# Splitting the first token-pair loads of a recurrence-and-mixer kernel between two issuing engines

## The chip, the core and the metric

The kernel runs on one core of a Trainium2 chip. The metric is the device time of one execution in microseconds (us). Beside plain runs there is one profiled execution, whose trace names every instruction, its engine and what it waited for.

## What is computed

The program is a gated linear recurrence followed by a token mixer and a channel MLP. Cut to what matters:

```python
# q, k, v, alpha: batch 4, heads 8, tokens 768, head size 48
for t in range(S):
    state = alpha[:, :, t, :, None] * state + einsum('bhd,bhe->bhde', k[:, :, t], v[:, :, t])
    y[:, :, t] = einsum('bhd,bhde->bhe', q[:, :, t], state)
x  = y with heads side by side            # (4, 768, 384)
u  = x + (x^T @ U @ V)^T                   # U: 768 x 32, V: 32 x 768
out = u + relu(u @ w_ch1) @ w_ch2          # 384 -> 1536 -> 384
```

## The kernel before

The 768 tokens of each batch are cut into six chunks of 128 tokens, written here as batch.chunk (q 1.1 is the q tensor of batch 1, chunk 1). A chunk needs four inputs: `alpha`, `k`, `q` and `v`, each 192 KB of float32 in one tile of a pool of 40 tiles named `io`. The 24 weight pieces (12 of `moe_w_ch1`, 12 of `moe_w_ch2`, also 192 KB each) and the results use the same pool.

Two forms of chunk exist. In batch 0 (all six chunks) and batch 1 (the first four) chunks are *paired*: a partition holds two neighbouring tokens of four heads, and the load reads runs of two tokens (line 322, "pload"). These are the token-pair loads, 40 in all; two of the first 36 are issued by ScalarE, the rest by SyncE. The other chunks are loaded a token to a partition (line 329).

For a paired chunk (`stage_pair`): ScalarE takes the logarithm of alpha (line 352); TensorE sums it over the tokens (lines 361 to 368); ScalarE takes exponentials (lines 375 to 377); VectorE or GpSimd multiply q and k by them (line 383, tile `rkq`); TensorE transposes both (line 400) and ScalarE or VectorE copy the result to `kqt`; TensorE forms the scores (line 424), VectorE masks them (line 435, tile `pm`), TensorE forms the state's increment (line 458), and the outputs (lines 497 and 507), which go to `xb` by way of `copy` (lines 263 to 267). `stage_mix` then builds u (lines 674 to 689) and its transpose `uT` (line 708), and `mlp1` and `mlp2` are the two large products (lines 737 and 763). Weight pieces are loaded at line 295 and cast to bf16 by `copy`.

The order of everything is written out by hand: `TABLE` is a string of three characters for each operation. The first two give the operation's number in base 64, the third the engine that runs it (P TensorE, A ScalarE, D VectorE, G GpSimd, S SyncE). `Plan.run` walks through it and emits the operations in that order; `SLOTS` gives the pool slot that each buffer takes when it is first used:

```python
op = self.ops[CODE.index(table[n]) * len(CODE) + CODE.index(table[n + 1])]
...
op.fn({"P": "PE", "A": "ACT", "D": "DVE", "G": "POOL", "S": "SP"}[table[n + 2]])
```

A load takes its issuing engine from that third letter:

```python
lambda e: (nc.scalar if e == "ACT" else nc.sync).dma_start(
    t().rearrange("p (h j) d -> p h (j d)", j=2), src[b, hs, sl, :].rearrange("h (p j) d -> p h (j d)", j=2)
),
```

Each engine works through its own list in that order. Waits between engines, and between a load and an earlier one that used the same semaphore, are put in when the program is built; loads and stores use eight semaphores (named DMAHW0 to DMAHW7 in the built program).

Of the kernel before, what the change touches and what calls it, by code (L numbers as in the profile page):

```python
# [13 lines left out]

CODE = "ABCDEFGHIJKLMNOPQRSTUVWXYZabcdefghijklmnopqrstuvwxyz0123456789+-"
TABLE = """
BISA8ABASA-AQgAA9SDjAA+SDlPBQSCcACePBKSCzABCSBBSC1PCdACfAABSChACgADnABDSCjDC4AC3ABJSCiDETABES++EClPDqGCkPBMSCnDEVPBRSC6G
CmDDsPBLSEYAC2ACrPDuABSSC5GCoPCsDDmABOSC8PEWACpDAFGC7PC0ABHSCtPCvPCqDC+ADCPDpGDKAC9DBFSCuDEXAC-PDDDBYSCwPEZGDADDEPDrPBUS
DMPDBDDtADkGDGPBGSDNACxDEaGDHPDFDDPADOADvPCyDBTSD8AEbPDIDDyPDJDDLGEcPDoADwDDZPD+PEeAEdDAGPEAABNSDzPDxDAHAEfPBPSD0DDQGEhD
BWSEDGGTABVSDaPAJPGqADbDAASDSPDRGD1PD-AGVPDUDEBAAKADcPD2DGsPGXADdDEUGDTPEgDGWABXSD3PECGEiPD4PEFPGuADVDEjPGtAD5PEHDD9GGvA  # L20
DWPGYABZSD7AGaGD6AEEPEkDElPBgSDYDELPEmPEGADePEMPBaSDXDGZGDfPEIPBcSENDDgPEJDADGEnPBbSDhAEPPGcPEpAEKDGbPDiAAQSEOPGUAEQPEoD
AMSGdAGeDGiPGwGERDEqPAOSESAGjDGfPHaAErPGkDGmPGyPGgDEsAGxGAUSHcPGhDASSE1PE7PHfAG0AE5PAWSE2DGnPHBAEzPE6DBdSGrGGpAGzPGoAEvP
E8DAeSG1AEtPHDPE0DAaSARAANGE9PEuDHGABeSE3PAPGE+AEwDG5PBkSG2PE4DHFAAVGAiSG6DExPHeAFXPHEAATGEyDFZPAXGG7DG9PFYDAgSFBPGlGG4D
FfPAfGFCAE-PHHDFgAAYSFJPG3DHdABiSFAAFdPBoSFaAFFPHIGFeDFKAAcSFhPFGAFHPHzABhSFDPFiAAhGBmSAjAH1PAZGFEDFbPBfSG8GH3AHJPH4AHKP
HhGFcAHLDFrPBlSFIAHMDFTPFsDFVPFUAAdGBjSHVPAbAHNPFWDHgGG+PHPDAmSFtPG-AH2AHODHjPH7GHAAFnPBqSIJAHlDFlPH5AAqSHCGFuDILPHiPFmD
AkSFRPINAH6GFoDHkAFjPFSAAoSHQPFkAHmPBpSHRDIMAH9PHoDH8PAwSHSGH-AFNPHbGHnDAySH+AHWPFpPFOAHTDIPGBnSHXPIAPAsSHYDHpPHZAICDFLP
# [802 lines left out]
```

## Time and profile before

| | |
|---|---|
| Runs | 159.76 us median of 3 (158.51 to 160.31) |
| Profiled execution | 158.96 us, of which the span of the trace is 157.2 us |
| Busy in the span | TensorE 147.3, VectorE 107.0, ScalarE 87.2, GpSimd 64.6 us |
| Moved | 31.64 MB, of which 28.62 MB on SyncE's queue (q1) and 2.75 MB on ScalarE's (q10) |
| Granted TensorE clock | full speed in every slice |

In the rows of the profile PE is TensorE, PEld its weight loads, DVE VectorE, ACT ScalarE, POOL GpSimd and SP SyncE. A name with a q (SPq, ACTq) is that engine's own list of instructions, on which loads are issued; the duration of such a row is the time of issuing, with any wait for a semaphore, and not that of the transfer. "To landing" is the time from the start of issuing until the data are there. Busy time of TensorE counts matmuls that overlap in its pipeline, so a row's mean is longer than the step from one matmul to the next.

### The profile page before, as it was taken

How to read it: one execution, taken by the hardware profiler on the slowest of the kernel's cores; microseconds unless marked ns; L12 is line 12 of the kernel's file. 1: busy time of each engine (PE TensorE's matmuls, PEld its weight loads, DVE VectorE, ACT ScalarE, POOL GpSimd, SP SyncE). 2: the span in 40 equal slices, each digit the busy share in tenths (PEclk: the TensorE clock that was granted, in tenths of full speed). 3: DMA queues.
4: the chain of work that ended last, by engine and by line, in shares of the span. 5: the costliest groups of instructions: out<-in, count | busy, mean ns of one | idle time of the engine just before them, and what ended most of it. 6: DMA issues, size and time to landing. Idle time of an engine off the chain costs nothing.

```text
span 157.2 us, 4460 instructions
## 1 busy us (share of the span) xinstructions
PE 147.3 (94%) x1708; PEld 97.5 (62%) x1708; DVE 107.0 (68%) x235; ACT 87.2 (55%) x226; POOL 64.6 (41%) x103
## 2 busy tenths in 40 slices
PE   0898998899999999999999999999999999999991
PEld 0567785566666656667667766666667565566561
DVE  6159998883878658986985948775798463435152
ACT  3858877869797636659788473358713102460000
POOL 8069865656868050275289246155412000000000
PEclk9999999999999999999999999999999999999999
DMA  5999889999999999899999899599780056875234
GB/s 124 323 327 320 230 198 253 277 311 278 251 264 293 246 266 219 151 200 238 206 238 169 139 231 135 116 209 217 145 198 23 0 104 160 263 222 135 74 126 174
DMA packets 99364, 31.64 MB, mean 201 GB/s; under 512 B 93040, under 2 KB 99312, under 8 KB 99344
## 3 DMA queue, kind: packets, MB, share of 16 engines
q1 hardware_dynamic: 85808, 28.62, 77.9%
q10 hardware_dynamic: 13536, 2.75, 9.1%
q8 instruction: 13, 0.21, 0.6%
q14 instruction: 7, 0.06, 0.1%
HBM read 23.89 MB, written 4.72 MB: 182 GB/s over the span
## 4 chain that ended last, share of the span: by engine, by line
PE 77%; SPq 14%; DMA 3%; ACT 1%; issue 1%; POOL 1%; DVE 1%; ACTq 0%
PE ps L763 30%; PE ps L737 29%; SPq L322 12%; DMA io<-in_alpha_dram 3%; PE ps L592 2%; PE ps L564 2%; PE ps L688 2%; PE ps L659 2%; PE ps L530 1%; PE ps L654 1%; PE ps L615 1%; PE ps L708 1%; SPq L270 1%; PE ps L674 1%; PE ps L400 1%
## 5 line engine op out<-in xcount | busy, mean ns | idle before, releaser
L763 PE MATMUL ps<-w_sb,h1t 128*128 128x384 bf16 (+2 forms) x300 | 53.2, 320 | 0.0
L737 PE MATMUL ps<-uT,w_sb 128*128 128x384 bf16 x288 | 51.2, 326 | 0.0
L747 ACT ACTIVATE h1t<-ps 128x384 bf16<-128x384 f32 x57 | 25.9, 501 | 20.9 <-PE ps L737 20.9
L763 PEld LDWEIGHTS <-h1t 128*128 128x128 bf16 x300 | 27.2, 97 | 16.1 <-issue 1.0
L737 PEld LDWEIGHTS <-w_sb 128*128 128x128 bf16 x288 | 27.0, 98 | 16.0
L749 DVE TENSOR_SCALAR h1t<-ps 128x384 bf16<-128x384 f32 x39 | 20.8, 554 | 12.5 <-PE ps L737 12.2
L769 DVE TENSOR_TENSOR io<-ub,ps 128x384 f32<-128x384 bf16 (+2 forms) x25 | 13.2, 536 | 11.3 <-PE ps L763 10.6
L602 DVE TENSOR_TENSOR pm<-ps,maskc 128x512 bf16<-128x512 f32 x28 | 17.7, 683 | 1.0 <-PE ps L592 0.8
L551 POOL TENSOR_TENSOR rkq<-io,ai 128x384 bf16<-128x384 f32 x11 | 10.2, 935 | 14.2 <-DMA io<-in_k_dram 6.6
L689 DVE TENSOR_TENSOR ub<-xb,ps 128x384 bf16<-128x384 bf16 x24 | 12.1, 551 | 2.8 <-PE ps L688 2.7
L551 POOL TENSOR_TENSOR rkq<-io,aa 128x384 bf16<-128x384 f32 x12 | 10.9, 912 | 7.1 <-PE ps L763 3.5
L435 DVE TENSOR_TENSOR pm<-ps,maskp 128x512 bf16<-128x512 f32 x20 | 13.1, 684 | 0.3
L263 ACT CAST xb<-ps 128x192 bf16<-128x192 f32 (+1 forms) x24 | 9.1, 402 | 5.9 <-DVE io L769 2.5
L383 POOL TENSOR_TENSOR rkq<-io,aa 128x384 bf16<-128x384 f32 x9 | 8.2, 918 | 9.2 <-ACT aa L376 4.1
L263 ACT COPY kqt<-ps 128x512 bf16<-128x512 bf16 x18 | 10.5, 595 | 1.5 <-PE ps L400 0.7
L626 POOL TENSOR_TENSOR st<-sm,tot 128x384 bf16<-128x384 f32 x6 | 5.0, 828 | 12.7 <-DVE sm L642 10.7
L267 POOL CAST w_sb<-io 128x384 bf16<-128x384 f32 x16 | 8.1, 514 | 4.6 <-DMA io<-in_moe_w_ch_dram 4.4
L541 ACT ACTIVATE aa<-ps 128x384 bf16<-128x384 f32 x14 | 6.9, 504 | 5.1 <-PE ps L532 4.4
L543 ACT ACTIVATE tot<-ps,off 128x4 f32<-128x4 f32 x22 | 5.9, 278 | 6.4 <-PE ps L532 6.4
L267 POOL CAST rv<-io 128x384 bf16<-128x384 f32 x17 | 8.8, 526 | 1.2 <-DMA io<-in_v_dram 1.1
L265 DVE COPY kqt<-ps 128x512 bf16<-128x512 bf16 x18 | 7.4, 418 | 2.9 <-PE ps L564 1.3
L400 PE MATMUL ps<-ident,rkq 128*128 128x128 bf16 x80 | 8.0, 232 | 1.3 <-ACT lt L352 0.6
(109 smaller groups left out, 214.8 us busy)
## 6 DMA issues: line engine op xcount, KB each, us to landing
io<-in_k_dram SPq DMA_DIRECT2D x24, 192.0 KB, 4.1
io<-in_q_dram SPq DMA_DIRECT2D x24, 192.0 KB, 4.4
io<-in_moe_w_ch_dram SPq DMA_DIRECT2D x24, 192.0 KB, 3.9
io<-in_alpha_dram SPq DMA_DIRECT2D x23, 192.0 KB, 4.2
io<-in_v_dram ACTq DMA_DIRECT2D x13, 192.0 KB, 4.2
out_dram<-io SPq DMA_DIRECT2D x13, 192.0 KB, 2.0
io<-in_v_dram SPq DMA_DIRECT2D x11, 192.0 KB, 3.8
out_dram<-io SPq DMA_DIRECT2D x20, 96.0 KB, 2.2
```

Of the source, the lines that this page charges most:

```text
L263: nc.scalar.copy(dst, src)
L267: nc.gpsimd.tensor_copy(dst, src)
L322: lambda e: (nc.scalar if e == "ACT" else nc.sync).dma_start(t().rearrange("p (h j) d -> p h (j d)", j=2), src[b, hs, sl, :].rearrange("h ...
L435: nc.vector.tensor_tensor(dst, s2, maskp.to_broadcast([C, 2, 2, C]), op=ALU.mult)
L551: eng.tensor_tensor(dst()[:, :, 0:D], a(), x(), op=ALU.mult)
L602: nc.vector.tensor_tensor(pm()[:, :, par, :], s2, maskc.to_broadcast([C, HP, C]), op=ALU.mult)
L689: P.add(f"u {b}.{c}", lambda e, c=c, hb=hb: nc.vector.tensor_tensor(ub()[:, c, :], xb()[:, c, :], hb()[:, 0:DM], op=ALU.add), r=[hb] + xk( ...
L737: nc.tensor.matmul(hb()[:, 0:TW], lhsT=w1_sb[:, ct, jt * 128 : (jt + 1) * 128], rhs=u_half(uT, ct, tt, b in QUEUE_U), start=(ct == 0), sto ...
L747: nc.scalar.activation(dst, hb()[:, 0:TW], AF.Relu)
L749: nc.vector.tensor_scalar_max(dst, hb()[:, 0:TW], 0.0)
L763: nc.tensor.matmul(hb()[:, 0 : hi - lo], lhsT=h1()[:, jt, c * C : (c + 1) * C], rhs=w2_sb[:, jt, lo:hi], start=(jt == 0), stop=(jt == NJ - 1),
L769: P.add(f"out_{hi - lo} {b}.{c}", lambda e, hb=hb, lo=lo, hi=hi: nc.vector.tensor_tensor(flat(ou)[:, lo:hi], ub()[:, c, lo:hi], hb()[:, 0 ...
```

## The change

Every second of the first 36 token-pair loads has the letter A in the place of S. Sixteen letters change; the two loads that were ScalarE's already keep theirs, so that 18 of the 36 are ScalarE's. The places in the table, the slots and all other operations stay. The moved loads, in the table's order, are q 0.0, q 0.3, k 0.1, k 0.3, alpha 0.4, v 0.3, q 0.4, k 0.2, alpha 1.0, v 0.5, v 0.4, k 1.0, k 1.1, q 1.1, v 1.1 and q 1.2. In the table:

```diff
-BISA8ABASA-AQgAA9SDjAA+SDlPBQSCcACePBKSCzABCSBBSC1PCdACfAABSChACgADnABDSCjDC4AC3ABJSCiDETABES++EClPDqGCkPBMSCnDEVPBRSC6G
-CmDDsPBLSEYAC2ACrPDuABSSC5GCoPCsDDmABOSC8PEWACpDAFGC7PC0ABHSCtPCvPCqDC+ADCPDpGDKAC9DBFSCuDEXAC-PDDDBYSCwPEZGDADDEPDrPBUS
+BISA8ABASA-AQgAA9SDjAA+ADlPBQSCcACePBKACzABCSBBAC1PCdACfAABSChACgADnABDSCjDC4AC3ABJACiDETABES++EClPDqGCkPBMACnDEVPBRSC6G
+CmDDsPBLAEYAC2ACrPDuABSSC5GCoPCsDDmABOAC8PEWACpDAFGC7PC0ABHSCtPCvPCqDC+ADCPDpGDKAC9DBFACuDEXAC-PDDDBYSCwPEZGDADDEPDrPBUA
...
```

The next rows of the table change alike: `BTS` (v 0.5), `BPS` (v 0.4), `BVS` (k 1.0), `BZS` (k 1.1), `BaS` (q 1.1), `BbS` (v 1.1) and `BeS` (q 1.2) end in A. The lists of TensorE, VectorE and GpSimd stay as they are; ScalarE's has 16 loads more and SyncE's 16 fewer.

More of the change, by code (lines that the diff above doesn't have):

```diff
@@ L16 @@
 TABLE = """
-BISA8ABASA-AQgAA9SDjAA+SDlPBQSCcACePBKSCzABCSBBSC1PCdACfAABSChACgADnABDSCjDC4AC3ABJSCiDETABES++EClPDqGCkPBMSCnDEVPBRSC6G
-CmDDsPBLSEYAC2ACrPDuABSSC5GCoPCsDDmABOSC8PEWACpDAFGC7PC0ABHSCtPCvPCqDC+ADCPDpGDKAC9DBFSCuDEXAC-PDDDBYSCwPEZGDADDEPDrPBUS
-DMPDBDDtADkGDGPBGSDNACxDEaGDHPDFDDPADOADvPCyDBTSD8AEbPDIDDyPDJDDLGEcPDoADwDDZPD+PEeAEdDAGPEAABNSDzPDxDAHAEfPBPSD0DDQGEhD
-BWSEDGGTABVSDaPAJPGqADbDAASDSPDRGD1PD-AGVPDUDEBAAKADcPD2DGsPGXADdDEUGDTPEgDGWABXSD3PECGEiPD4PEFPGuADVDEjPGtAD5PEHDD9GGvA
-DWPGYABZSD7AGaGD6AEEPEkDElPBgSDYDELPEmPEGADePEMPBaSDXDGZGDfPEIPBcSENDDgPEJDADGEnPBbSDhAEPPGcPEpAEKDGbPDiAAQSEOPGUAEQPEoD
+BISA8ABASA-AQgAA9SDjAA+ADlPBQSCcACePBKACzABCSBBAC1PCdACfAABSChACgADnABDSCjDC4AC3ABJACiDETABES++EClPDqGCkPBMACnDEVPBRSC6G
+CmDDsPBLAEYAC2ACrPDuABSSC5GCoPCsDDmABOAC8PEWACpDAFGC7PC0ABHSCtPCvPCqDC+ADCPDpGDKAC9DBFACuDEXAC-PDDDBYSCwPEZGDADDEPDrPBUA
+DMPDBDDtADkGDGPBGSDNACxDEaGDHPDFDDPADOADvPCyDBTAD8AEbPDIDDyPDJDDLGEcPDoADwDDZPD+PEeAEdDAGPEAABNSDzPDxDAHAEfPBPAD0DDQGEhD
+BWSEDGGTABVADaPAJPGqADbDAASDSPDRGD1PD-AGVPDUDEBAAKADcPD2DGsPGXADdDEUGDTPEgDGWABXSD3PECGEiPD4PEFPGuADVDEjPGtAD5PEHDD9GGvA
+DWPGYABZAD7AGaGD6AEEPEkDElPBgSDYDELPEmPEGADePEMPBaADXDGZGDfPEIPBcSENDDgPEJDADGEnPBbADhAEPPGcPEpAEKDGbPDiAAQSEOPGUAEQPEoD
 AMSGdAGeDGiPGwGERDEqPAOSESAGjDGfPHaAErPGkDGmPGyPGgDEsAGxGAUSHcPGhDASSE1PE7PHfAG0AE5PAWSE2DGnPHBAEzPE6DBdSGrGGpAGzPGoAEvP
-E8DAeSG1AEtPHDPE0DAaSARAANGE9PEuDHGABeSE3PAPGE+AEwDG5PBkSG2PE4DHFAAVGAiSG6DExPHeAFXPHEAATGEyDFZPAXGG7DG9PFYDAgSFBPGlGG4D
+E8DAeSG1AEtPHDPE0DAaSARAANGE9PEuDHGABeAE3PAPGE+AEwDG5PBkSG2PE4DHFAAVGAiSG6DExPHeAFXPHEAATGEyDFZPAXGG7DG9PFYDAgSFBPGlGG4D
 FfPAfGFCAE-PHHDFgAAYSFJPG3DHdABiSFAAFdPBoSFaAFFPHIGFeDFKAAcSFhPFGAFHPHzABhSFDPFiAAhGBmSAjAH1PAZGFEDFbPBfSG8GH3AHJPH4AHKP
```

## The prediction

> **What bounds the kernel now.** I read the chain that ended last first, then the chain in order of time, then the busy time by stretch, then the engines' own rows around 28 us. The page's chain:
>
> ```profile
> PE 77%; SPq 14%; DMA 3%; ACT 1%; issue 1%; POOL 1%; DVE 1%; ACTq 0%
> PE ps L763 30%; PE ps L737 29%; SPq L322 12%; DMA io<-in_alpha_dram 3%; PE ps L592 2%; PE ps L564 2%; PE ps L688 2%; PE ps L659 2%; PE ps L530 1%; PE ps L654 1%; PE ps L615 1%; PE ps L708 1%; SPq L270 1%; PE ps L674 1%; PE ps L400 1%
> ```
>
> Two stages show here: a long one that TensorE sets, and an opening whose chain is SyncE issuing the token-pair loads (line 322). In order of time the opening ends so (start us, us, what):
>
> ```profile
> 23.42 5.30 DMA io<-in_alpha_dram
> ```
>
> and at the same moment GpSimd waits for the q load that was issued just before (start, duration, engine, line, what; in brackets the idle time and what ended it):
>
> ```profile
> 28.37 0.91 POOL L383 TENSOR_TENSOR rkq<-io,aa 128x384 bf16<-128x384 f32 x1 [2.60 <-DMA io<-in_q_dram]
> ```
>
> The busy time by stretch (stretch: length, PE, PEld, DVE, ACT, POOL busy, granted clock, DMA share, GB/s):
>
> ```profile
> 7.90:15.70 7.80, 7.20 (x145) 5.50 (x144) 5.78 (x15) 5.40 (x16) 6.53 (x8) 1.00 1.17 323
> 15.70:23.60 7.90, 7.90 (x190) 6.17 (x188) 7.66 (x20) 6.42 (x21) 5.98 (x10) 1.00 0.86 214
> 23.60:31.40 7.80, 6.51 (x136) 4.50 (x129) 6.82 (x16) 6.00 (x17) 4.49 (x7) 1.00 0.97 265
> 31.40:120.00 88.60, 88.38 (x989) 58.03 (x986) 67.08 (x132) 57.85 (x150) 44.23 (x65) 1.00 1.02 210
> 120.00:157.20 37.20, 33.99 (x244) 21.01 (x240) 16.45 (x33) 6.76 (x16) 0.13 (x1) 1.00 0.47 133
> ```
>
> The reader is to see three things. After 31.4 us TensorE is busy 88.38 of 88.60 us and its order is fixed, so a microsecond lost before 31.4 is hardly ever given back, and one gained there is kept. In the opening no engine has much room: VectorE 7.66 of 7.90, ScalarE 6.42 of 7.90. And 323 GB/s over 7.8 us looks like the ceiling of the transfers: a load of 192 KB (196.6 thousand bytes) takes 0.61 us of it.
>
> **What the change does to the order.** Of the 36 loads two were ScalarE's already; sixteen more go there. The change keeps each load's place in the program, but an engine works through its own list. SyncE loses sixteen items and runs ahead, into the weight loads; a load on ScalarE goes out only when ScalarE has come to it. Beyond that, the compiled program gives the loads eight semaphores in turn and lets each load wait until the one eight places ahead has landed, over both queues. The places are those of the build's merged order, and that order has changed (places from 0, read from the two compiled programs; chunks are written batch.chunk):
>
> ```
> load     place before -> after   after: waits for place
> v 0.5        24 -> 33             25 (second half of U)
> v 0.4        26 -> 39             31 (first weight)
> k 1.0        28 -> 42             34 (weight)
> k 1.1        32 -> 48             40 (weight)
> q 1.1        34 -> 51             43 (alpha of a single chunk)
> v 1.1        36 -> 53             45 (weight)
> alpha 1.2    35 -> 30             22 (q 0.4)
> 1st weight   37 -> 31             23
> ```
>
> So the last pair loads that the opening needs stand 13 to 17 places later, behind weights that nobody needs yet, and the waiting instruction is on ScalarE: every activation and copy behind it waits too.
>
> **The terms.** What SyncE did, and what a landing takes:
>
> ```profile
> 2.33 0.51 SPq L322 DMA_DIRECT2D io<-in_q_dram  x1
> ...
> 14.28 1.15 SPq L322 DMA_DIRECT2D io<-in_v_dram  x1
> ...
> 21.77 0.51 SPq L322 DMA_DIRECT2D io<-in_k_dram  x1
> ...
> 22.87 0.51 SPq L322 DMA_DIRECT2D io<-in_q_dram  x1
> ```
>
> ```profile
> DMA to landing us min/median/max: 2.9/4.2/5.3
> ```
>
> An issue without a wait takes 0.51 us; the one of 1.15 holds a wait for a semaphore.
>
> *Issuing on ScalarE.* Sixteen times 0.51 is 8.2 us of ScalarE's sequencer. ScalarE has issued loads before:
>
> ```profile
> 52.41 0.52 ACT L263 CAST w_sb<-io 128x384 bf16<-128x384 f32 x1
> 52.55 0.40 ACTq L329 DMA_DIRECT2D io<-in_v_dram  x1
> 52.82 0.52 ACT L263 CAST rv<-io 128x384 bf16<-128x384 f32 x1
> ```
>
> The two casts start 0.41 us apart with an issue of 0.40 us between: it ran under the first cast. The bounds are 0 and 8.2 us; I take 0 by this row, since nearly every moved issue follows an activation of about 0.5 us that covers it. Without that cover (ScalarE waiting, queue empty) each costs its 0.51. SyncE's saved 8.2 us are worth nothing by themselves while the transfers are at their ceiling.
>
> *The start.* q 0.0 went out at 2.33; now it follows the first Ln on ScalarE.
>
> ```profile
> 3.98 0.94 ACT L352 ACTIVATE lt<-io 128x384 bf16<-128x384 f32 x2 [0.82 <-DMA io<-in_alpha_dram]
> 7.25 0.56 DVE L383 TENSOR_TENSOR rkq<-io,aa 128x384 bf16<-128x384 f32 x1 [3.05 <-ACT aa L376]
> ```
>
> 4.0 + 4.2 = 8.2 against VectorE's start at 7.25: the first product is 0.95 us late. It is no term of its own: the later hold is longer, and takes its place.
>
> *The hold on ScalarE.* I carry every load through the rule "issued when its engine is there and the load eight places ahead has landed", with 4.2 us to land and 0.55 us between SyncE's issues. The rows of ScalarE that tell when it would be there:
>
> ```profile
> 11.29 0.90 ACT L375 ACTIVATE ai<-ps 128x384 bf16<-128x384 f32 x2
> ...
> 15.27 0.51 ACT L376 ACTIVATE aa<-ps 128x384 bf16<-128x384 f32 x1
> 15.64 0.54 ACT L352 ACTIVATE lt<-io 128x384 bf16<-128x384 f32 x1
> ...
> 18.21 0.94 ACT L352 ACTIVATE lt<-io 128x384 bf16<-128x384 f32 x2 [0.40 <-DMA io<-in_alpha_dram]
> ...
> 23.51 0.78 ACT L263 CAST xb<-ps 128x192 bf16<-128x192 f32 x3 [0.95 <-PE ps L507]
> ...
> 26.47 0.52 ACT L352 ACTIVATE lt<-io 128x384 bf16<-128x384 f32 x1 [0.71 <-DMA io<-in_alpha_dram]
> ...
> 28.80 0.52 ACT L352 ACTIVATE lt<-io 128x384 bf16<-128x384 f32 x1 [0.47 <-DMA io<-in_alpha_dram]
> ```
>
> q 0.0 goes out at 4.0 and lands at 8.2; q 0.5 on SyncE waits for it and lands at 12.4; q 0.4 on ScalarE waits for that one, where ScalarE would have been after the first Exp of 11.29, at 11.7: about +1.0 with the issue. v 0.5 waits for the second U load, issued 13.5, landed 17.7, where ScalarE stands at 16.6 with that delay (15.27, 0.4 and 1.0): the Ln of 15.64 starts at 17.75 (+2.1). v 0.4 waits for the first weight, issued 17.15, landed 21.35: the Ln of 18.21 at 21.4 (+3.2). k 1.0 waits for a weight issued 18.3: 22.5 (+3.9). k 1.1: 26.1 for 21.77. q 1.1: 27.25 for 22.87. v 1.1: 28.35; the casts of 23.51 begin at 28.4 (**+4.9**). q 1.1 then lands at 31.45, where GpSimd began with it at 28.37 (+3.1). Behind the last cast stand the mixer's first product, the chain to `uT` and the first MLP matmul:
>
> ```profile
> 32.42 1.14 PE L737 MATMUL ps<-uT,w_sb 128*128 128x384 bf16 x6
> ```
>
> Of the two alpha waits above (0.71 and 0.47) those loads, now early, give back about 0.7. With 4.2 us a landing the opening ends **4.2 us** late.
>
> *Is 4.2 right?* In that order eight loads are nearly always under way: 8 x 196.6 / 4.2 gives 374 GB/s, more than the 323 that the rows reach. At 323 GB/s place 43, for which q 1.1 waits, lands no sooner than 3.9 + 43 x 0.61 - 1.1 (three loads are short) = 29.0, q 1.1 itself at 33.2: 4.8 late. And in the middle of the opening a landing took longer:
>
> ```profile
> io<-in_alpha_dram SPq DMA_DIRECT2D x4, 192.0 KB, 5.1
> ```
>
> (alpha loads issued from 12 to 24 us: their number, size, median us to landing). v 1.1 stands behind six landings in a row on its semaphore, so 0.1 us more on each is 0.6 us at the end. With 4.4 the end is 1.2 later than with 4.2: 5.4; 4.8 by the ceiling; I take **+5.5** for the opening with the queue at its ceiling, and nothing back later, since TensorE is busy 88.38 of 88.60 us. Bounds: 3.7 us a landing gives 4.2 - 3.0 = +1.2; 4.9 gives 4.2 + 4.2 = +8.4.
>
> *Sum.* The profiled execution took 158.96 us: 158.96 + 5.5 = 164.5 us. The median of the runs shown is 159.76, 0.8 above it; I leave the sum where it is. One per cent, about what a measurement of this kernel tells from no change, is 1.6 us.
>
> **Rivals.**
>
> *SyncE freed: faster.* The chain of the opening is SyncE's issues; with half of them gone alpha 1.2 goes out near 16.6 and not at 23.42, the weights come early, and TensorE's gaps before 31.4 close. They are 0.60 + 0 + 1.29 us in the three stretches after 7.9: 158.96 - 1.9 = 157.1. It decides if ScalarE is never held for over about 1 us, the slack of 0.95 it has at 23.51. For it: the alpha row of 5.30 us. Against it: the q that comes at the same moment is ScalarE's now, and the transfers are at 323 GB/s. [...] Chance 0.04.
>
> *ScalarE's loads land sooner.* A second queue with one or two loads in it might be served ahead of its share, so that landings fall to 3.6 us: 4.9 - 6 x 0.6 = +1.3 on ScalarE, 160.3. The rows so far speak against it:
>
> ```profile
> io<-in_v_dram ACTq DMA_DIRECT2D x13, 192.0 KB, 4.2
> ...
> io<-in_v_dram SPq DMA_DIRECT2D x11, 192.0 KB, 3.8
> ```
>
> [...] Chance 0.10.
>
> *The hold feeds itself.* ScalarE late makes its loads late, SyncE's loads wait for those, and landings stay near the 5.1 of the middle, at 5.0: 4.2 + 6 x 0.8 = +9, 168.0, more if the second batch's loads follow. For it: 214 GB/s between 15.7 and 23.6, with waits for semaphores on SyncE. Against it: once ScalarE is held, fewer loads are under way. Chance 0.10.
>
> **How the numbers follow.** The forecast has the remaining 0.76, with its own range 161.0 to 167.5. The range for 8 in 10 is 160.8 to 168.8: it holds the forecast and most of the self-feeding hold, and leaves out the faster rival and the quick landings (0.14) and the far end. Faster by over 1%: 0.03, all from the first rival. Within 1%: 0.09, 0.01 from the first and 0.08 from the second. Slower: 0.88.
>
> **What would show it.** Right: ScalarE issues on its queue of well over 1 us between 15 and 30 us, k 1.1, q 1.1 and v 1.1 issued after 25 us, the alpha load of 1.2 and the first weights issued before 19 us, GpSimd waiting for k and q of 1.1, the first MLP matmul near 38 and not 32.4, and nearly the same time from there to the end. Wrong: ScalarE's issues all near 0.5 us, or VectorE and TensorE no later at 30 us than before; or landings well under 4 us; or a late opening that is made up before 120 us.

## The result, and the profile after

The changed kernel takes 167.84 us (median of 4 runs, 166.57 to 168.13); the kernel before took 160.03 beside it (158.51 to 160.63). The ratio is 1.052, with a 95% interval of 1.048 to 1.057: slower by some 8 us (7.8 by the medians, which alone give 1.049), where 164.5 (160.8 to 168.8) was forecast. Ratios here and below leave out runs that took over 1.5% more than the fastest of the same kernel (among them one of the four of e1 and three of the six of e9). The profiled execution took 166.57 us with a span of 164.8; before it was 158.96 and 157.2, so the two traces differ by 7.6 us.

Where they part is seen at the first MLP matmul, which stood at 32.42 us:

```profile
40.47 1.14 PE L737 MATMUL ps<-uT,w_sb 128*128 128x384 bf16 x6
```

That is 8.05 us later. From there to the end of the span it was 157.2 - 32.42 = 124.8 us; now it is 164.8 - 40.47 = 124.3. The loss is made in the opening, and 0.5 us of it comes back. By stretch (stretch: length, PE, PEld, DVE, ACT, POOL busy, granted clock, DMA share, GB/s):

```profile
7.90:15.70 7.80, 4.88 (x92) 3.18 (x91) 4.46 (x10) 4.05 (x11) 5.94 (x7) 1.00 1.17 323
15.70:23.60 7.90, 6.19 (x114) 4.65 (x110) 4.66 (x12) 4.20 (x11) 3.27 (x6) 0.57 1.10 297
23.60:31.40 7.80, 7.07 (x144) 5.38 (x141) 5.65 (x13) 4.15 (x13) 4.41 (x7) 0.78 1.10 329
31.40:39.30 7.90, 6.48 (x131) 4.57 (x129) 6.77 (x16) 5.72 (x17) 4.04 (x8) 1.00 1.02 249
39.30:128.00 88.70, 88.44 (x999) 58.44 (x996) 67.09 (x133) 57.84 (x150) 43.97 (x64) 1.00 0.86 175
```

Up to 31.4 us VectorE, ScalarE and GpSimd do less than before in each stretch (ScalarE 4.20 and 4.15 from 15.7 us on, where it did 6.42 and 6.00); TensorE does too up to 23.6, and its 7.07 after that is work at a lower clock. The transfers do more from 15.7 us on: 297 and 329 GB/s, where they did 214 and 265. The engines wait and the transfers are busy with something that nobody needs yet. The column before the last two is news: the granted clock, 1.00 everywhere before, is 0.57 and 0.78 here.

The chain that ended last has changed its kind, from SyncE's issues (SPq 14%) to landings (DMA 16%):

```profile
PE 77%; DMA 16%; ACT 1%; issue 1%; DVE 1%; POOL 1%; SPq 1%; ACTq 0%
```

In order of time (start us, us, what) the opening is a row of landings, with an issue between:

```profile
4.02 4.46 DMA io<-in_q_dram
...
8.50 4.80 DMA io<-in_q_dram
...
13.32 4.40 DMA io<-in_q_dram
17.74 0.37 SPq L322
...
18.70 4.36 DMA io<-in_moe_w_ch_dram
...
23.12 5.71 DMA io<-in_moe_w_ch_dram
28.85 0.38 ACTq L322
```

q 0.0, then q 0.5, then q 0.4, then alpha 1.2, whose issue lets the first weights out behind it, two weights in turn, and only then k 1.1 on ScalarE. Two of the five landings are weights, which the opening doesn't use. ScalarE's own list shows who pays (start, duration, engine, line, what; in brackets the idle time and what ended it):

```profile
20.05 0.38 ACTq L322 DMA_DIRECT2D io<-in_v_dram  x1
20.48 0.52 ACT L352 ACTIVATE lt<-io 128x384 bf16<-128x384 f32 x1 [2.29 <-DMA ue_in<-in_moe_U_dram]
...
24.15 0.37 ACTq L322 DMA_DIRECT2D io<-in_k_dram  x1
24.57 0.52 ACT L352 ACTIVATE lt<-io 128x384 bf16<-128x384 f32 x1 [1.06 <-DMA io<-in_moe_w_ch_dram]
...
28.85 0.38 ACTq L322 DMA_DIRECT2D io<-in_k_dram  x1
29.27 0.54 ACT L263 CAST xb<-ps 128x192 bf16<-128x192 f32 x2 [1.53 <-DMA io<-in_moe_w_ch_dram]
...
30.63 0.37 ACTq L322 DMA_DIRECT2D io<-in_q_dram  x1
31.64 0.38 ACTq L322 DMA_DIRECT2D io<-in_v_dram  x1
32.05 0.76 ACT L263 CAST xb<-ps 128x192 bf16<-128x192 f32 x3 [1.75 <-PE ps L400]
```

Two logarithms that need neither U nor a weight wait, one 2.29 us for U and the other 1.06 us for a weight. The reader is to see why: the load in front of each (v 0.5, k 1.0) waits for that landing, and stands in ScalarE's list. The last bracket names TensorE, but the cast starts 0.03 us after the issue of v 1.1 has ended (31.64 + 0.38), so that load let it go. The chain passes this one by: it runs from k 1.1 over the cast of 29.27, TensorE and VectorE's mask to a cast at 32.27.

### The profile page after: what moved, and what is told of

It is laid out like the page before. It is cut to its first block, busy times and chain, and to the rows that moved or that the text cites. A ratio compares the mean times of both kernels' runs of the same rounds, so it can differ in the third digit from the quotient of the medians.

```text
span 164.8 us, 4455 instructions
## 1 busy us (share of the span) xinstructions
PE 150.0 (91%) x1708; PEld 99.2 (60%) x1708; DVE 107.3 (65%) x235; ACT 87.6 (53%) x226; POOL 64.9 (39%) x103
## 2 busy tenths in 40 slices
DMA packets 99364, 31.64 MB, mean 192 GB/s; under 512 B 93040, under 2 KB 99312, under 8 KB 99344
## 3 DMA queue, kind: packets, MB, share of 16 engines
q10 hardware_dynamic: 21984, 5.90, 15.6%
## 4 chain that ended last, share of the span: by engine, by line
PE 77%; DMA 16%; ACT 1%; issue 1%; DVE 1%; POOL 1%; SPq 1%; ACTq 0%
PE ps L763 29%; PE ps L737 29%; DMA io<-in_q_dram 8%; DMA io<-in_moe_w_ch_dram 6%; PE ps L688 2%; PE ps L592 2%; PE ps L564 2%; DMA io<-in_alpha_dram 2%; PE ps L659 2%; PE ps L530 1%; PE ps L654 1%; PE ps L615 1%; PE ps L424 1%; PE ps L674 1%; PE ps L708 1%; PE ps L400 1%
## 5 line engine op out<-in xcount | busy, mean ns | idle before, releaser
L551 POOL TENSOR_TENSOR rkq<-io,ai 128x384 bf16<-128x384 f32 x11 | 10.3, 941 | 18.8 <-ACT ai L540 12.4
L267 POOL CAST rv<-io 128x384 bf16<-128x384 f32 x17 | 9.6, 571 | 3.6 <-DMA io<-in_v_dram 3.6
L400 PE MATMUL ps<-ident,rkq 128*128 128x128 bf16 x80 | 8.5, 244 | 1.6 <-POOL rkq L383 1.2
L361 PE MATMUL ps<-lt,upto 128*128 128x384 bf16 x10 | 4.3, 428 | 6.2 <-ACT lt L352 6.2
```

The lines of the kernel that those rows point to most:

```text
L267: nc.gpsimd.tensor_copy(dst, src)
L400: nc.tensor.matmul(dst, lhsT=ring()[:, HP * j + 2 * a : HP * j + 2 * a + 2, :].rearrange("t h w -> t (h w)"), rhs=ident, start=True, stop= ...
L551: eng.tensor_tensor(dst()[:, :, 0:D], a(), x(), op=ALU.mult)
```

## The experiments

Two theories stood at first. **Place**: the late pair loads come late because weights stand ahead of them, and each load waits for the landing eight places ahead; who issues them matters little. **ScalarE**: the loads come late because they stand behind ScalarE's activations. A third came up with the trace: the **clock**, halved for some 10 us.

### Weights held behind v 1.1 (e1_gate)

```diff
+    P.add("gate", lambda e: nc.scalar.copy(io.slots[34][:, 0, 0:2], off))
# table, right behind v 1.1:
-...BbA...
+...BbAQhA...
```

Slot 34 is that of the first weight, so its load now waits for a copy of two columns that stands behind v 1.1. The sixteen loads stay on ScalarE.

> The changed kernel, with one small ScalarE copy behind its last load of batch 1 (v 1.1) into the tile that the first weight load fills: SyncE can't run ahead into the weights, and in the compiled order the pair loads stand before all weights again (k 1.1 at place 34, q 1.1 at 35, v 1.1 at 36, where the changed kernel has 48, 51 and 53). Theory (turns behind weights hold ScalarE): the holds at v 0.4, k 1.0, k 1.1, q 1.1 and v 1.1 go, ScalarE's loads of 1.1 leave before 26 us, the first MLP matmul comes at 34 to 37 us and the time is 161 to 164 us. Rival (issuing on ScalarE itself, or the place in its list, costs the time): the same 16 loads are on ScalarE at the same places, so 166 to 168 us.

161.74 us, ratio 1.0155 (1.010 to 1.021). SyncE's weights, v 1.1 on ScalarE and the first MLP matmul:

```profile
26.41 2.72 SPq L295 DMA_DIRECT2D io<-in_moe_w_ch_dram  x6
```

```profile
25.62 0.52 ACTq L322 DMA_DIRECT2D io<-in_v_dram  x1
```

```profile
34.48 1.14 PE L737 MATMUL ps<-uT,w_sb 128*128 128x384 bf16 x6
```

v 1.1 goes out 6.0 us earlier than in the changed kernel, and the MLP begins 6.0 us earlier, with the same loads on the same engine. That is inside what the theory of place gave, and well under its rival. Of the 8.05 us, 6 belong to the weights that had moved ahead.

### The changed order, all on SyncE (e5_sync_order)

The sixteen letters go back to S, and the operations are put in the order that the changed kernel's build gave (the table below is its beginning); the slots are given out beforehand, so that each buffer keeps its own.

```diff
-BISA8ABASA-AQgAA9SDjAA+SDlPBQSCcACePBKSCzABCSBBSC1PCdACfAABSChACgADnABDSCjDC4AC3ABJSCiDETABES++EClPDqGCkPBMSCnDEVPBRSC6G
+A8ABISA-ABASQgAA9SDjABQSA+SDlPCcACePBCSBKSCzAABSBDSBBSC1PCdACfAChACgADnACjDC4AC3ABESBRSBSSBJSCiDETA++EClPDqGCkPBHSBMSCnD
+        order = "".join(ORDER.split())   # the table before, for the slots alone
+        for n in range(0, len(order), 3):
+            ...
+                    b.slot = b.pool.slots[CODE.index(next(nxt))]
```

> The kernel before, with all moved loads still issued by SyncE, but SyncE's list put into the merged order that the changed kernel's build has up to v 1.1 (two weights before v 0.5, six before v 0.4, eight before k 1.0, and so on); slots as before. It takes ScalarE out and keeps the late places. Theory A (the late place among the loads costs the time, whoever issues): k 1.1, q 1.1 and v 1.1 leave after 25 us, the first MLP matmul comes at 36 to 39 us, 163 to 166.5 us. Theory B (what costs is ScalarE standing at the wait with its other work behind it): at most 161.5 us, since only the consumers of the late loads wait.

169.71 us, ratio 1.0685 (1.063 to 1.074): slower than the changed kernel and than the theory of place gave, with none of the moved loads on ScalarE. (Lines are shifted by 36: 358 is the load, 388 the logarithm, 419 `rkq`, 773 the MLP.)

```profile
23.07 0.94 ACT L388 ACTIVATE lt<-io 128x384 bf16<-128x384 f32 x2 [4.68 <-DMA io<-in_alpha_dram]
```

```profile
35.67 0.91 POOL L419 TENSOR_TENSOR rkq<-io,ai 128x384 bf16<-128x384 f32 x1 [3.37 <-DMA io<-in_k_dram]
```

```profile
43.90 1.14 PE L773 MATMUL ps<-uT,w_sb 128*128 128x384 bf16 x6
```

Here nobody waits for an issue on ScalarE; ScalarE and GpSimd wait for the data themselves, alpha and k of batch 1. ScalarE's standing isn't needed for a loss of this size. The path is another one, though: the chain up to 23 us is SyncE's run of issues, some 0.5 us each, and the profile names no landing that SyncE waits for before 40 us.

```profile
18.24 1.60 SPq L358 DMA_DIRECT2D io<-in_alpha_dram  x3
19.89 0.98 SPq L331 DMA_DIRECT2D io<-in_moe_w_ch_dram  x2
```

The granted clock is lower too, 0.64 from 23.6 to 31.4 us and 0.79 from 31.4 to 39.3 us. So e5 shows that late places alone can cost this much, and not what the changed kernel would lose without ScalarE's standing.

### One half of the letters each (e2_first9, e3_last7)

e2 changes the first nine letters (q 0.0 to alpha 1.0), e3 the last seven (v 0.5 to q 1.2).

```diff
# e2: first lines of the table as changed; v 0.5, v 0.4, k 1.0, k 1.1, q 1.1, v 1.1, q 1.2 keep S
-...A+S ... BKS ... BBS ... BJS ... BMS ... BLS ... BOS ... BFS ... BUS...
+...A+A ... BKA ... BBA ... BJA ... BMA ... BLA ... BOA ... BFA ... BUA...
# e3: the first nine keep S
-...BTS ... BPS ... BVS ... BZS ... BaS ... BbS ... BeS...
+...BTA ... BPA ... BVA ... BZA ... BaA ... BbA ... BeA...
```

> Only the first nine of the sixteen loads (q 0.0 to alpha 1.0) on ScalarE, the last seven back on SyncE. Theory: no weight stands before a pair load, so the holds late in the opening go; what is left is q 0.0 late, q 0.5 behind it and q 0.4 behind that, a hold of about 1.7 us on ScalarE near 13 us: 160.5 to 162.5 us. Rival (cost by number of issues on ScalarE): 9/16 of 8 us, 164 to 165. Second rival (TensorE's granted clock halves after the gap near 13 to 15 us, and that costs the time): the gap stays, so the clock falls again and 163 to 166.

> Only the last seven of the sixteen (v 0.5 to q 1.2) on ScalarE. In the compiled order their places are now early (v 0.5 at 18, v 0.4 at 23), before loads of SyncE that wait for them: k 0.4 on SyncE stands at 26 and waits for v 0.5, which leaves only when ScalarE is there (about 15 us). Theory (whoever's turn comes behind a late load of the other queue is held): here SyncE is held, k 0.4 leaves near 19.5 us instead of 15.5, and 162 to 164.5 us. Rival (cost by number of issues): 7/16 of 8 us, 163 to 164; but then SyncE's issues show no hold of over 1.5 us.

e2 took 162.52 us, ratio 1.022 (1.017 to 1.028), with the first MLP matmul at 35.26; e3 160.29, ratio 1.010 (1.007 to 1.013), with it at 34.16. e2 came out at the upper edge of its theory (160.5 to 162.5). Its granted clock fell to 0.81 between 15.7 and 23.6 us, so a part of its loss may be the clock; that wasn't tried. For e3 the mechanism was seen, but the time lies below the numbers of both its theory and its rival: SyncE, which is not freed much by these seven, waits for ScalarE's v 0.5.

```profile
14.20 0.51 SPq L322 DMA_DIRECT2D io<-in_q_dram  x1
19.12 0.37 SPq L322 DMA_DIRECT2D io<-in_k_dram  x1
```

That is 4.4 us in which SyncE issues nothing, and so it doesn't run ahead into the weights either: they go out from 24.22 us on. The halves cost 3.5 and 1.6 us against the 158.8 beside them, 5.1 together; the whole costs 7.8 (8.3 by its ratio). The rest is probably their joint work: the first nine set SyncE free to reach the weights, the last seven are the loads that these pass. No run separates it further.

### The clock (e4_warm)

Eight and seven matmuls whose results nobody uses stand in two gaps of TensorE of the changed kernel.

```diff
+++I   # ahead of the 61st operation of the table
+++H   # ahead of the 103rd
```

> The changed kernel with 8 and 7 filler matmuls of TensorE (512 columns, result unused) put into the two gaps of its opening, near 13 to 15 and 19 to 21 us. It tests whether the granted clock of 0.5 between 17 and 27 us, seen in the changed kernel alone, costs time. Theory (the end of the opening is set by landings in turn, ending with k 1.1 leaving at 28.85 us): clock near 1.0, time within 1 us of the changed kernel, 166.5 to 168.5. Rival (the clock is part of the loss): 164 to 166.

The clock in the stretch from 15.7 to 23.6 us went from 0.57 to 0.78, and from 23.6 to 31.4 from 0.78 to 1.00 (third column from the end):

```profile
15.70:23.60 7.90, 5.99 (x88) 3.89 (x79) 4.21 (x10) 2.66 (x8) 2.27 (x3) 0.78 1.01 266
23.60:31.40 7.80, 6.43 (x143) 4.69 (x140) 5.51 (x13) 5.42 (x17) 5.06 (x7) 1.00 1.07 324
```

That is not all of the clock, but over half of what was lost. The time stayed: 167.37 us, ratio 1.053 (1.050 to 1.056), the first MLP matmul at 41.14 us. In the changed kernel the clock is a companion, as far as e4 tells: TensorE is waiting there anyway.

### q 0.0 alone, and everything but q 0.0 (e7_only_q00, e8_after_q00)

```diff
# e7: of the sixteen letters only this one is changed; e8: all but this one
-...A+S...
+...A+A...
```

> The kernel before with q 0.0 alone on ScalarE. Its place stays early; alpha 0.4 on SyncE waits for it (8.4 us instead of 8.2). VectorE's first product starts near 8.4 instead of 7.25. Theory (in e1 it is the wait on ScalarE behind q 0.5 that costs, not q 0.0's own lateness): 158.5 to 160.3 us, at most 1 us over before. Rival (the late start itself is kept through the opening): 160.5 to 161.5.

> The changed kernel with q 0.0 back on SyncE, the other fifteen on ScalarE, no gate. The early hold goes as in e6, the weights still stand before k 1.0, k 1.1, q 1.1 and v 1.1 (places 40, 46, 50, 52). If the two holds add up, 2 us less than the changed kernel: 165 to 166.5. If the late landings in turn alone set the end of the opening, no less: 166.5 to 168.

q 0.0 alone gives 158.54 us, ratio 1.000 (0.996 to 1.004), first MLP matmul at 32.11. Without it the change gives 167.83, ratio 1.056 (1.050 to 1.063), first MLP matmul at 41.18. The first load of the changed kernel's chain can be put back, and the next one, q 0.3, takes its place in the chain. The chain of e8 is not otherwise the same: from 20 to 27 us it is TensorE's own work, at a granted clock of 0.56 up to 23.6 us and 0.79 after it. So the equal time doesn't show by itself that q 0.0 costs nothing within the change.

### The gate without q 0.0, and fillers behind the gate (e6, e10, e9)

e6 is e1 with q 0.0 back on SyncE. e10 is e6 with three and six filler matmuls, e9 is e1 with eight.

```diff
# e6, against e1:   A+A -> A+S
# e10, against e6:  +++D ahead of the 61st operation, +++G ahead of the 103rd
# e9, against e1:   +++I ahead of the 61st operation
```

> The gate of e1 (no weight load before v 1.1 has been issued), and q 0.0 back on SyncE; the other fifteen loads stay on ScalarE. e1 kept a hold near 13 us: q 0.0 leaves at 3.8, q 0.5 waits for it, q 0.4 on ScalarE waits for q 0.5. Theory (that chain is the rest): q 0.4 leaves before 12 us, first MLP matmul at 32.5 to 34 us, 158.8 to 160.5 us, the same as before or within 1%. Rival (fifteen issues on ScalarE cost by themselves): as e1, near 161.7.

> The kernel with the gate and q 0.0 back on SyncE, with three filler matmuls before 12.9 us and six near 18 us; nothing else is changed. Without them the granted clock was 0.50 from 15.7 to 24 us, the first MLP matmul stood at 36.61 us, and the kernel took 163.5. Theory A (the half clock makes this one slower than the gate alone, since its opening ends in TensorE's own work): clock 0.9 or more over 16 to 24 us, first MLP matmul at 34 to 35.2, time 160.8 to 162.2. Theory B (its other order of landings, k 0.4 and v 0.5 behind q 0.3, k 0.3 and q 1.0, is what costs): first MLP matmul at 36.2 or later, time 163 to 164.

> The kernel with the gate (weights held until v 1.1 has landed), and eight filler matmuls on TensorE in the gap of 12.6 to 14.6 us in which it waited for the copy of v 0.5's neighbour on ScalarE; nothing else is changed. With the gate alone the granted clock fell to 0.50 and 0.82 between 16 and 20 us, the first MLP matmul stood at 34.48 us, and the kernel took 161.74 against 158.8. Theory A (what is left of the loss behind the gate is the half clock, because the early transfers no longer hold anything after 20 us): clock 1.0 from 14 to 20 us, first MLP matmul 33.0 to 33.8, time 159.8 to 161.0. Theory B (what is left is the hold of the loads between 12 and 16 us, and the clock is only its companion, as it was in the changed kernel itself): first MLP matmul at 34.3 to 34.8, time 161.4 to 162.2.

e6 was a surprise: 163.5 us, ratio 1.030 (1.026 to 1.035), slower than e1, and outside of what either theory gave. Its chain is other landings, and after these TensorE's own work at half clock. e10 has the same chain of landings (the row of 13 us, of e6 and then of e10):

```profile
13.12 5.82 DMA io<-in_q_dram
```

```profile
13.00 5.94 DMA io<-in_q_dram
```

and in the stretch behind it, e6 first and then e10, with the clock in the third column from the end:

```profile
12.00:15.70 3.70, 2.42 (x62) 1.97 (x60) 3.13 (x9) 2.29 (x5) 3.46 (x5) 0.99 1.17 323
15.70:23.60 7.90, 6.24 (x94) 4.25 (x92) 3.89 (x10) 5.09 (x14) 3.68 (x6) 0.50 0.95 243
23.60:31.40 7.80, 7.80 (x192) 6.26 (x189) 6.70 (x17) 5.61 (x18) 5.37 (x8) 0.86 0.49 130
```

```profile
12.00:15.70 3.70, 3.11 (x68) 2.19 (x67) 3.32 (x9) 2.18 (x5) 3.56 (x5) 1.00 1.17 324
15.70:23.60 7.90, 6.56 (x120) 4.53 (x120) 4.86 (x13) 5.48 (x16) 3.86 (x7) 1.00 0.99 255
23.60:31.40 7.80, 7.80 (x208) 5.93 (x206) 7.59 (x18) 6.50 (x23) 5.76 (x9) 1.00 0.70 193
```

The same group of four transposes near 17 us shows the price of the half clock, e6 and then e10:

```profile
17.35 0.61 PE L400 MATMUL ps<-ident,rkq 128*128 128x128 bf16 x4
```

```profile
17.02 0.40 PE L400 MATMUL ps<-ident,rkq 128*128 128x128 bf16 x4
```

e10 took 160.66 us, ratio 1.011 (1.008 to 1.015), its first MLP matmul at 34.33 where e6 had it at 36.61: 2.3 us of e6 were the clock, by the times 2.8. So no cost of the clock was seen in the changed kernel, where data are late, and 2 to 3 us where TensorE sets the pace.

e9 decides less: ratio 1.017 (1.011 to 1.024). Its six runs lie between 160.93 and 164.26 us, the profiled one at 163.59, so its trace is not read here. Its two fastest runs took 160.93 and 161.12 us at a granted clock of 0.997 and 1.0 over the span, another took 163.0 at 0.979; that points to the clock, but it can't be called shown.

No kernel here was faster than the one before; q 0.0 alone was the same.

## Why the prediction was right, and where its size was off

**The bound.** Right. A loss before the MLP is kept: 8.05 us at the first MLP matmul, 7.6 in the span.

**The order and its waits.** Right, and the cause. All six waits of the prediction's table are in the trace: v 0.5, v 0.4, k 1.0, k 1.1, q 1.1 and v 1.1 each go out 0.02 or 0.03 us after the landing that the table names. alpha 1.2 and the first weights went out before 19 us, as said:

```profile
16.04 2.07 SPq L322 DMA_DIRECT2D io<-in_alpha_dram  x2
18.15 4.07 SPq L295 DMA_DIRECT2D io<-in_moe_w_ch_dram  x6
```

With those weights behind v 1.1 (e1) 6 of the 8 us are gone; with the same order on SyncE alone (e5) there is more than all of the loss, though by another path. The prediction put weight on ScalarE being held. That is the form the loss takes here; the late data are nearly as late by themselves, since q 1.1 lands at 36.10 us and GpSimd begins with it at 36.26, 7.9 us later than before.

**Issuing on ScalarE at 0.** Right where ScalarE has work:

```profile
14.18 0.50 ACT L263 CAST rv<-io 128x384 bf16<-128x384 f32 x1
14.53 0.37 ACTq L322 DMA_DIRECT2D io<-in_k_dram  x1
14.58 0.59 ACT L263 COPY kqt<-ps 128x512 bf16<-128x512 bf16 x1
```

The cast and the copy start 0.40 us apart with an issue of 0.37 between, as far as before the change, where none stood between such a pair (12.04 and 12.44 us). An issue on ScalarE was also shorter than the 0.51 us of the prediction: 0.37 or 0.38 us from 13 to 32 us. And e1, with all sixteen still on ScalarE, bounds what issuing there could cost at the 1.6% that it has left.

**The start.** "No term of its own" agrees with the runs: q 0.0 alone costs nothing (e7), and the change without it takes the same time (e8), by a chain that differs. In the trace of the changed kernel q 0.0 heads the chain, which would have misled a reader of the chain alone.

**The hold.** The steps came in the order forecast, each later than forecast. The forecast times are those worked out with 4.2 us a landing, but for the last row, which has the +5.5 of the sum (us):

| | forecast | measured |
|---|---|---|
| q 0.4 issued | 12.4 | 13.32 |
| logarithm behind v 0.5 | 17.75 | 20.48 |
| v 0.4 issued | 21.35 | 22.56 |
| k 1.0 issued | 22.5 | 24.15 |
| k 1.1 issued | 26.1 | 28.85 |
| q 1.1 issued | 27.25 | 30.63 |
| v 1.1 issued | 28.35 | 31.64 |
| casts behind it | 28.4 | 32.05 |
| first MLP matmul | near 38 | 40.47 |

**The term that was too small** is the landing time. The forecast took 4.4 us a landing, a value for which it gave no row, and +5.5, a little over the 5.4 and 4.8 that it had worked out. The pair loads of the changed kernel:

```profile
DMA to landing us min/median/max: 3.3/4.8/6.4
```

The five landings on the chain took 4.46, 4.80, 4.40, 4.36 and 5.71, 4.75 in the mean. Put into the prediction's own formula, 4.2 + 6 x (4.8 - 4.2) = 7.8 us, against 8.05 measured at the first MLP matmul and 7.6 in the time. The step that was mis-sized is thus "*Is 4.2 right?*": the ceiling of 323 GB/s was weighed there, but from it only +4.8 was drawn, by place 43 alone. What it means for every landing was not drawn: with eight loads of 196.6 thousand bytes always under way at 323 GB/s (329 was the most that a stretch of this kernel reached), one takes 8 x 0.61 = 4.9 us, and the trace has 4.8. Counted from the issue and landing times of the two traces, 7.4 to 7.9 loads were under way in each of the three stretches from 7.9 to 31.4 us, where before it was 5.7 to 6.3. The nearest size was that of the rival "the hold feeds itself" (5.0 a landing, 168.0), given 0.10. Its reason is seen too: in the chain SyncE's q 0.5 waits until 8.50 us for ScalarE's q 0.0, and alpha 1.2 until 17.74 for q 0.4. What spoke against it, fewer loads under way once ScalarE is held, did not come.

**The rivals.** SyncE freed gave no gain: alpha 1.2 did go out at 17.74 and not at 23.42, and nothing was earned by it. On the whole ScalarE's loads did not land sooner than SyncE's in the opening; those of k did, those of v landed later (5 to 32 us; their number, size, median us to landing):

```profile
io<-in_k_dram ACTq DMA_DIRECT2D x5, 192.0 KB, 4.5
io<-in_k_dram SPq DMA_DIRECT2D x4, 192.0 KB, 5.1
...
io<-in_v_dram ACTq DMA_DIRECT2D x4, 192.0 KB, 5.2
...
io<-in_v_dram SPq DMA_DIRECT2D x3, 192.0 KB, 4.8
```

These rows show no favour for the shorter queue. Over all token-pair loads issued there the median is 4.8 us on either queue (13 and 15 loads), with 2.3 loads under way on ScalarE's in the mean and 5.4 on SyncE's.

**What would show it.** ScalarE's issue rows between 15 and 30 us were to be well over 1 us; they are 0.37 or 0.38, because the wait is not in them: it is in the idle time ahead of the next activation (2.29, 1.06, 1.53 us). By the letter a sign of being wrong (issues all near 0.5 us) came true while ScalarE was held: contrary to what is said ahead of the prediction, these rows do not hold the wait for a landing. k 1.1's row begins at 28.85, when the landing that it waited for has ended (23.12 + 5.71). The issue of 1.15 us at 14.28 in the kernel before was read as such a wait too; the load eight places ahead had landed at 13.23, so what made it long is open. GpSimd was to wait for k and q of 1.1; it did for k:

```profile
32.85 0.91 POOL L383 TENSOR_TENSOR rkq<-io,ai 128x384 bf16<-128x384 f32 x1 [1.18 <-DMA io<-in_k_dram]
36.26 0.91 POOL L383 TENSOR_TENSOR rkq<-io,aa 128x384 bf16<-128x384 f32 x1 [2.50 <-PE ps L507]
```

For q 1.1, which landed at 36.10 us, it did not: by then TensorE was the later one, by 0.1 us.

**What stays open.** With the gate, q 0.0 on SyncE and a full clock 1.1% is left (e10). The first MLP matmul stands 1.9 us late there, and the chain has a landing of 5.94 us for q 1.0; whether that landing or the new order of the first loads is what costs was not tried by itself.

## What to carry to other kernels

Before moving a DMA to another engine, write down the merged order of all DMAs and which landing each one waits for: here SyncE, set free, ran on to its next loads (the first weight went out at 18.15 us and not at 24.53), and as the loads share semaphores in turn these stood ahead of the ones that were moved (k 1.1 went out at 28.85 us and not at 21.77). Where the transfers run at the most that a stretch showed (323 to 329 GB/s in this opening), price a landing as loads under way x bytes / that rate (here 8 x 0.61 = 4.9 us, where the trace has 4.8), not by the median of a profile in which fewer were under way, and multiply by the number of landings that follow one another. With few under way the product was too small: in e1 there were 2.3 between 21.6 and 26.4 us (2.3 x 0.61 = 1.4 us), and the loads issued then landed in 2.45 to 3.01 us. What is to be moved ahead is data that is needed sooner; data that isn't needed yet can be held back with a small dependence (it gave back 6 of the 8 us lost here).

## What the runs showed of the hardware that was not expected

The granted clock of TensorE halved without any long gap. In e6 TensorE was busy 2.42 of the 3.70 us up to 15.7 us, its two longest gaps there were these,

```profile
12.95 0.35 PE L458 MATMUL ps<-rv,rkq 64*128 64x96 bf16 x8 [0.55 <-ACT rv L263]
...
14.95 0.38 PE L400 MATMUL ps<-ident,rkq 128*128 128x128 bf16 x4 [0.60 <-ACT aa L376]
```

and the clock was 0.50 for the next 7.9 us; with 3.11 busy of the 3.70 (e10) it stayed at 1.00. Whether the busy share is what decides, and at which share, was not tried. The changed kernel in 40 slices of 4.12 us shows the same dip:

```profile
PEclk9999557999999999999999999999999999999999
```

In e6 the clock fell at 15.6 us, and from TensorE's first matmul there, at 4.5 us, no gap was over 0.6 us by then. The dip was worth 2.3 us at the first MLP matmul where TensorE set the pace (e6 against e10), and no gain was seen from mending most of it where TensorE was waiting for data (e4).
